# Sign words of the weight conversion formed on GpSimd beside VectorE's operations on h

## The chip, the cores and the metric

The kernel runs on one core of a Trainium2 chip. The metric is the device time of one execution in microseconds (us); the median of three runs is given. Engines are named as in the profile: PE is TensorE, PEld its weight load, DVE is VectorE, ACT is ScalarE, POOL is GpSimd, SP is SyncE, which here only issues DMAs.

## The reference

Linear attention over 8 batches and 8 heads, an RMS norm, and a feed-forward layer whose activation is a rational function:

```
kv = einsum('bhsd,bhse->bhde', k, v);  out = einsum('bhsd,bhde->bhse', q, kv)
x  = (out / sqrt(mean(out^2) + 1e-6) * g_norm)  -> 4608 x 512, float32
h  = x @ w_in                          # 512 -> 2048
P  = a0 + a1*h + a2*h^2 + a3*h^3
Q  = 1 + |b0|*|h| + |b1|*h^2
y  = (P / (Q + 1e-6)) @ w_out          # 2048 -> 512
```

The activations are float32, but `w_in` and `w_out` arrive as float64. They reach the chip as pairs of 32-bit words and are turned into float32 there.

## The kernel before

**Tiles and slots.** The 4608 tokens are cut into 9 tiles of 512 (`t`), the 2048 hidden columns into 16 chunks of 128 (`c`). One pair (t, c) is a slot, and the loop over `slots` (line 594) runs through all 144, tile by tile; slot i of tile 0 is chunk i. The order within each engine's queue is the order in which the code issues the instructions (`manual_schedule`). In a slot the first product of the next slot (`gemm1`, h), the second product of the slot two before (`gemm2`, into `acc`) and a piece of the next tile's attention (`att_kv`, `att_o`, ...) are issued for PE, and the rational function of the slot itself for ACT and DVE.

**The rational function.** For a slot, `ew_a` has ACT write d = h^2 (L427), q = |b0 h| (L428) and u (L430), and DVE form q (L429, the denominator) and u (L431, times h). `ew_b` has DVE go on with u and h (L437), while ACT takes d = exp(-ln q) (L438, L439). `ew_c` corrects the quotient on DVE: L443 (q and d), L445 (u and d), L451 (the result g). `ew_b` and `ew_c` take a `fill` function, by which other DVE work is placed between their operations: `fill(-1)` stands ahead of L437, `fill(0)` behind L443, `fill(2)` behind L451. The h that these read lies in PSUM, everything else in SBUF. In tile 0 the products are plain float32, so `ew_d` (the split of g into two parts, L461 and L462) does nothing there.

**The weight conversion.** The weights come in 16 units of two chunks each (`schedule`, line 125: the slot of the fetch, of `conv_a`, of `conv_b`, of the split). `conv_a` on ACT scales the high word, read as float32, by 2^-112, and the low word by 2^-29 (L183), both in place. `conv_b` on DVE makes the float32: `conv_b1` (L197) shifts the high word left by 3, `conv_b2` puts the sign bit of the high word back (L202) and adds the scaled low word as an integer (L203). Three units are converted ahead of the loop or in slot 0, in halves (`part`). The other 13 are converted whole, one in each of the slots 1 to 13: L197 stands at `fill(-1)`, between L431 and L437, and L202 and L203 at `fill(0)`, behind L443. The code of one slot of the loop around it:

```
        for u in at_slot(2, i):
            rest[-1].append(lambda u=u: conv_b1(u))
            rest[0].append(lambda u=u: conv_b2(u))
        ew_b(t, c, ph, lambda k: [f() for f in rest[k]])
```

**Names.** `raw_wi`, `raw_wo` are the fetched words, `wiw`, `wow` the float32 weights of tile 0 (`ups`), `parts`, `wil`, `wol` the two-part weights that the later tiles use (`split_w`, L224 and L231), `kvl` the small part of the kv matrix (L249), `op` the attention product (L327), `kvp` the kv product (L301).

Of the kernel before, what the change touches and what calls it, by code (L numbers as in the profile page):

```python
# [9 lines left out]
I32 = mybir.dt.int32  # L10
# [3 lines left out]
ALU = mybir.AluOpType  # L14
# [9 lines left out]
def linear_attention_then_rational_ffn(  # L24
# [13 lines left out]
    PE, ACT, DVE, POOL = nc.tensor, nc.scalar, nc.vector, nc.gpsimd  # L38
# [38 lines left out]
    b1abs = const.tile([P, 1], F32, name="b1abs")  # L77
# [41 lines left out]
    def f32(t):  # L119
        return t.bitcast(F32)  # L120
# [27 lines left out]
    def at_slot(step, k):  # L148
        return [u for u in units if schedule[u][step] == k]
# [7 lines left out]
    raws, ups, w32, whl, gparts = {}, {}, {}, {}, {}  # L157
# [15 lines left out]
    def words(u, part):  # L173
        w = raws[u].bitcast(I32).rearrange("p (f w) -> p f w", w=2)[:, part]
        return w[:, :, 0], w[:, :, 1]

    both, one, two = slice(0, 2 * DM), slice(0, DM), slice(DM, 2 * DM)
# [7 lines left out]
    def conv_a(u, part=both, engine="S"):  # L185
        low, high = words(u, part)
        scale(engine, f32(high), f32(high), 2.0**-112)
        scale(engine, low, low.bitcast(U32), 2.0**-29)

    def conv_b1(u, part=both):  # L190
        kind, c = u
        low, high = words(u, part)
        if u not in ups:
            ups[u] = wpool.tile([P, 2 * DM], F32, tag=f"f{units.index(u)}", name=f"{kind}w{c}")
            for j in range(2):
                w32[kind, c + j] = ups[u][:, j * DM:(j + 1) * DM]
        DVE.tensor_scalar(ups[u].bitcast(I32)[:, part], high, 3, None, ALU.logical_shift_left)  # L197

    def conv_b2(u, part=both):
        low, high = words(u, part)  # L200
        w = ups[u].bitcast(I32)[:, part]
        DVE.scalar_tensor_tensor(w, high, -(1 << 31), w, ALU.bitwise_and, ALU.bitwise_or)  # L202
        DVE.tensor_tensor(w, w, low, ALU.add)  # L203

    def conv_b(u, part=both):
        conv_b1(u, part)
        conv_b2(u, part)
# [6 lines left out]
    def split_w(u):  # L214
        kind, c = u
        i = units.index(u)
        w = ups.pop(u)
        if i == NU - 1:
            last = work.tile([P, 2 * DM], F32, tag="rb", name="w_last", bufs=2)
            DVE.tensor_copy(last, w)  # L220
            w = last
        fpart = lambda k, what: wpool.tile([P, 2 * DM], F32R, tag=f"f{k}", name=f"{kind}{what}{c}")
        wh = fpart(i - 1, "h") if i == NU - 1 else gpart((i + 1) // 2, (i + 1) % 2)
        ACT.copy(wh, w)  # L224

        def rest():
            wl = gpart(0, 0) if i == 0 else fpart(i if i == NU - 1 else i - 1, "l")
            for j in range(2):
                js = slice(j * DM, (j + 1) * DM)
                whl[kind, c + j] = wh[:, js], wl[:, js]  # L230
            DVE.tensor_tensor(wl, w, f32(wh), ALU.subtract)  # L231
        return rest
# [171 lines left out]
    def gemm1(t, c):  # L404
        ph = ps_h.tile([P, TW], F32, tag="h", name=f"h_{t}_{c}")
        gemm1_part(t, c, ph, slice(0, TW))
        return ph

    def gemm1_part(t, c, ph, cs):
        for kc in range(NPAIR):  # L410
            ks = slice(kc * P, (kc + 1) * P)
            if t == 0:
                PE.matmul(ph, w32["wi", c][:, ks], x0[:, kc, cs], start=(kc == 0), stop=(kc == NPAIR - 1))  # L413
                continue
            xh, xl = (f[:, cs] for f in x[t][kc])
            wh, wl = (f[:, ks] for f in whl["wi", c])
            PE.matmul(ph, wh, xl, start=(kc == 0), stop=False)  # L417
            PE.matmul(ph, wl, xh, start=False, stop=False)  # L418
            PE.matmul(ph, wh, xh, start=False, stop=(kc == NPAIR - 1))  # L419


    def ew_a(t, c, ph, w=TW):
        nm = f"{t}_{c}"
        d = work.tile([P, w], F32, tag="d", name=f"d_{nm}")
        q = work.tile([P, w], F32, tag="q", name=f"q_{nm}")
        u = work.tile([P, w], F32, tag="u", name=f"u_{nm}")
        ACT.activation(d, ph, AF.Square)  # L427
        ACT.activation(q, ph, AF.Abs, scale=b0)  # L428
        DVE.scalar_tensor_tensor(q, d, b1abs, q, ALU.mult, ALU.add)  # L429
        ACT.activation(u, ph, AF.Identity, bias=na[:, 2:3], scale=na[:, 3:4])  # L430
        DVE.tensor_tensor(u, u, ph, ALU.mult)  # L431
        pend[t, c] = (d, q, u)

    def ew_b(t, c, ph, fill=lambda k: None):
        d, q, u = pend[t, c]
        fill(-1)
        DVE.scalar_tensor_tensor(u, u, na[:, 1:2], ph, ALU.add, ALU.mult)  # L437
        ACT.activation(d, q, AF.Ln, bias=bias[:, 2:3], scale=QSC)  # L438
        ACT.activation(d, d, AF.Exp, bias=bias[:, 3:4], scale=-1.0)  # L439
# [14 lines left out]
    def ew_d(t, c, w=TW):  # L454
        u = pend.pop((t, c))[2]
        if (t, c) in gs:
            return
        nm = f"{t}_{c}"
        gh = work.tile([P, w], F32R, tag="gh", name=f"gh_{nm}")
        gl = work.tile([P, w], F32R, tag="gl", name=f"gl_{nm}")  # L460
        ACT.copy(gh, u)  # L461
        DVE.tensor_tensor(gl, u, f32(gh), ALU.subtract)  # L462
        gs[t, c] = (gh, gl)

    def gemm2(t, c, subs=range(NSUB)):
        g = gs.pop((t, c))
        c = int(c)
        if c == 0:
            acc[t] = [ps_acc.tile([P, DM], F32, tag="acc", name=f"acc_{t}_{s}") for s in range(NSUB)]
        for k, s in enumerate(subs):  # L470
            ss = slice(k * P, (k + 1) * P)
            o = acc[t][s]
            if unsplit(t, c):
                PE.matmul(o, g[:, ss], w32["wo", c], start=(c == 0), stop=(c == NF - 1))  # L474
                continue
            gh, gl = g
            wh, wl = whl["wo", c]
            PE.matmul(o, gl[:, ss], wh, start=(c == 0), stop=False)  # L478
            PE.matmul(o, gh[:, ss], wl, start=False, stop=False)  # L479
            PE.matmul(o, gh[:, ss], wh, start=False, stop=(c == NF - 1))  # L480

    def evacuate(t):
        for k in range(NSUB // 2):
            ob = work.tile([P, 2, DM], F32, tag="rb", name=f"ob_{t}_{k}", bufs=2)
            for s in range(2):
                ACT.copy(ob[:, s], acc[t][2 * k + s])
            r0 = t * TW + 2 * k * P
            nc.sync.dma_start(out[r0:r0 + 2 * P].rearrange("(s p) d -> p s d", s=2), ob)
# [101 lines left out]


    slots = [(t, c) for t in range(NTILE) for c in range(NF)]
    ph = gemm1(0, 0)
    for i, (t, c) in enumerate(slots[:-1]):
        ew_a(t, c, ph)
        if i:
            ew_d(*slots[i - 1])
        rest = {-1: [], 0: [], 1: [], 2: []}
        if i == 0:
            rest[0].append(lambda: conv_b(units[2], two))  # L600
        for u in at_slot(2, i):
            rest[-1].append(lambda u=u: conv_b1(u))
            rest[0].append(lambda u=u: conv_b2(u))
        ew_b(t, c, ph, lambda k: [f() for f in rest[k]])
        for u in at_slot(3, i):
            rest[2].append(split_w(u))
        for u in at_slot(1, i):
            conv_a(u)
        if i >= LAG:
            gemm2(*slots[i - LAG])  # L610
            if slots[i - LAG][1] == NF - 1:
                evacuate(slots[i - LAG][0])
        if i < 4:
            ph = gemm1(0, i + 1)
        if t + 1 < NTILE:
            for step, p in (attention0 if t == 0 else attention)[c]:
                todo_dve = step(t + 1, p)
                if todo_dve:
                    rest[2 if t == 0 else fillat[step]].append(todo_dve)
            for u in at_slot(0, i):  # L620
                fetch_w(u)
        if 4 <= i < len(slots) - 2:
            ph = gemm1(*slots[i + 1])
        if c == NF - 2 and t < NTILE - 1:
            xl = [split(t + 1, p) for p in range(NPAIR)]
            for k in range(2):
                rest[k].append(xl[k])
                rest[2].append(xl[2 + k])
        ew_c(t, c, lambda k: [f() for f in rest[k]])
# [43 lines left out]
```

## Time and profile before

| | |
|---|---|
| median of three runs | 917.49 us (917.32 to 918.82) |
| the profiled execution | 916.91 us, of it the span 915.1 us |
| PE busy | 900.0 us (98%) |
| DVE busy | 800.3 us (87%) |
| ACT busy | 685.6 us (75%) |
| POOL busy | 4.8 us (1%), all of it in the first 20 us |
| granted PE clock | 1.00 throughout |

Busy PE is not PE at its peak: a matmul's end is modelled, and instructions that follow each other overlap by some tenths of a microsecond. So the time from one instruction's start to the next one's is the better measure of a step, on DVE too. The chain of waits is followed back from the last instruction; where an engine stands in it, that engine set the pace.

### The profile page before, as it was taken

To read this page: it belongs to the slowest core of one execution; us is meant where nothing else is said; L and a number is where in the kernel's file an instruction comes from. 1 tells how busy PE (TensorE), PEld (TensorE's weight loads), DVE (VectorE), ACT (ScalarE), POOL (GpSimd) and SP (SyncE) were. 2 spreads that over 40 slices of the span, in tenths; PEclk is the share of its full clock that TensorE was granted. 3 is DMA by queue.
4 is the path that set the end of the run, shared out by engine and by line. 5 is a ranking of instruction groups with operands and counts; after the bars stand their busy time and mean duration, and the time that the engine had idled before them with its cause. 6 is when DMAs were issued, how large, how long until landed. Compare 5 with 4: busy or idle time off the path is not lost.

```text
span 915.1 us, 11641 instructions
## 1 busy us (share of the span) xinstructions
PE 900.0 (98%) x4292; PEld 680.5 (74%) x4292; DVE 800.3 (87%) x1251; ACT 685.6 (75%) x1163; POOL 4.8 (1%) x32
## 2 busy tenths in 40 slices
PE   7999999999999999999999999999999999999998
PEld 5444445777678788878887888788887888788886
DVE  3799999999988899889987997889878988898887
ACT  2687866988687778777877787678867787777665
POOL 2000000000000000000000000000000000000000
PEclk9999999999999999999999999999999999999999
DMA  8945101322032013212221213110311020101001
GB/s 321 368 178 218 35 24 41 96 72 48 1 127 71 20 39 103 65 41 47 87 81 41 48 41 124 44 48 29 98 52 48 0 69 13 48 1 46 1 1 46
DMA packets 24416, 65.89 MB, mean 72 GB/s; under 512 B 2792, under 2 KB 2792, under 8 KB 24360
## 3 DMA queue, kind: packets, MB, share of 16 engines
q1 hardware_dynamic: 23328, 64.10, 21.5%
q10 hardware_dynamic: 1032, 1.05, 0.3%
q8 instruction: 33, 0.54, 0.3%
q14 instruction: 23, 0.19, 0.1%
HBM read 55.58 MB, written 9.57 MB: 71 GB/s over the span
## 4 chain that ended last, share of the span: by engine, by line
PE 83%; DVE 11%; ACT 3%; issue 1%; DMA 1%; DVEq 0%; ACTq 0%
PE h L417 13%; PE h L419 12%; PE h L418 12%; PE acc L478 12%; PE acc L479 11%; PE acc L480 11%; PE acc L474 3%; PE h L413 2%; PE kvp L301 2%; DVE q L429 1%; DVE u L445 1%; DVE q L443 1%; PE idle L532 1%; DVE u L437 1%; PE ms L345 1%
## 5 line engine op out<-in xcount | busy, mean ns | idle before, releaser
L427 ACT ACTIVATE d<-h 128x512 f32<-128x512 f32 x143 | 85.8, 600 | 160.5 <-PE h L419 146.7
L417 PE MATMUL h<-x,parts 128*128 128x512 f32 (+1 forms) x516 | 205.7, 399 | 0.0
L419 PE MATMUL h<-x,parts 128*128 128x512 f32 (+1 forms) x516 | 200.5, 389 | 0.0
L479 PE MATMUL acc<-wol,gh 128*128 128x512 f32 x492 | 191.5, 389 | 0.7 <-DVE wol L231 0.7
L429 DVE SCALAR_TENSOR_TENSOR q<-d,b1abs,q 128x512 f32<-128x512 f32 x143 | 107.1, 749 | 81.3 <-ACT q L428 81.1
L418 PE MATMUL h<-x,wil 128*128 128x512 f32 (+1 forms) x452 | 175.5, 388 | 0.0
L478 PE MATMUL acc<-parts,gl 128*128 128x512 f32 x440 | 171.6, 390 | 0.2 <-DVE gl L462 0.2
L480 PE MATMUL acc<-parts,gh 128*128 128x512 f32 x440 | 171.2, 389 | 0.0
L438 ACT ACTIVATE d<-q,bias 128x512 f32<-128x512 f32 x143 | 105.2, 735 | 29.8 <-DVE q L429 28.8
L417 PEld LDWEIGHTS h<-x,parts 128*128 128x128 f32 x516 | 96.9, 188 | 26.3 <-DVE gl L462 5.0
L419 PEld LDWEIGHTS h<-x,parts 128*128 128x128 f32 x516 | 96.9, 188 | 20.6
L430 ACT ACTIVATE u<-h,na 128x512 f32<-128x512 f32 x143 | 112.2, 784 | 0.0
L479 PEld LDWEIGHTS acc<-wol,gh 128*128 128x128 f32 x492 | 92.3, 188 | 20.0 <-DVE wol L231 1.0
L439 ACT ACTIVATE d<-d,bias 128x512 f32<-128x512 f32 x143 | 103.5, 724 | 4.7
L445 DVE SCALAR_TENSOR_TENSOR u<-u,na,d 128x512 f32<-128x512 f32 x143 | 106.5, 745 | 0.0
L437 DVE SCALAR_TENSOR_TENSOR u<-u,na,h 128x512 f32<-128x512 f32 x143 | 106.0, 742 | 0.3
L443 DVE SCALAR_TENSOR_TENSOR q<-q,d 128x512 f32<-128x512 f32 x143 | 98.4, 688 | 1.3 <-ACT d L439 1.3
L431 DVE TENSOR_TENSOR u<-u,h 128x512 f32<-128x512 f32 x143 | 97.9, 684 | 0.9
L428 ACT ACTIVATE q<-h,ab 128x512 f32<-128x512 f32 x143 | 98.1, 686 | 0.0
L418 PEld LDWEIGHTS h<-x,wil 128*128 128x128 f32 x452 | 85.0, 188 | 16.2 <-issue 0.2
L478 PEld LDWEIGHTS acc<-parts,gl 128*128 128x128 f32 x440 | 82.6, 188 | 18.4 <-DVE gl L462 1.1
L480 PEld LDWEIGHTS acc<-parts,gh 128*128 128x128 f32 x440 | 82.6, 188 | 17.2
(136 smaller groups left out, 1089.8 us busy)
## 6 DMA issues: line engine op xcount, KB each, us to landing
kvm<-in_kv_dram SPq DMA_DIRECT2D x28, 640.0 KB
raw_wo<-in_w_out_dram SPq DMA_DIRECT2D x8, 1024.0 KB
qr<-in_qT_dram SPq DMA_DIRECT2D x32, 256.0 KB
out_dram<-ob SPq DMA_DIRECT2D x16, 512.0 KB
rb<-rd SPq DMA_DIRECT2D x28, 256.0 KB
raw_wi<-in_w_in_dram SPq DMA_DIRECT2D x6, 1024.0 KB
first<-in_first_dram SPq DMA_DIRECT2D x4, 640.0 KB
raw_wi<-in_w_in_dram SPq DMA_DIRECT2D x4, 512.0 KB
```

Source lines behind the costliest of these rows:

```text
L417: PE.matmul(ph, wh, xl, start=(kc == 0), stop=False)
L418: PE.matmul(ph, wl, xh, start=False, stop=False)
L419: PE.matmul(ph, wh, xh, start=False, stop=(kc == NPAIR - 1))
L429: DVE.scalar_tensor_tensor(q, d, b1abs, q, ALU.mult, ALU.add)
L430: ACT.activation(u, ph, AF.Identity, bias=na[:, 2:3], scale=na[:, 3:4])
L437: DVE.scalar_tensor_tensor(u, u, na[:, 1:2], ph, ALU.add, ALU.mult)
L438: ACT.activation(d, q, AF.Ln, bias=bias[:, 2:3], scale=QSC)
L443: DVE.scalar_tensor_tensor(q, q, QEPS, d, ALU.add, ALU.mult)
L445: DVE.scalar_tensor_tensor(u, u, na[:, 0:1], d, ALU.add, ALU.mult)
L478: PE.matmul(o, gl[:, ss], wh, start=(c == 0), stop=False)
L479: PE.matmul(o, gh[:, ss], wl, start=False, stop=False)
L480: PE.matmul(o, gh[:, ss], wh, start=False, stop=(c == NF - 1))
```

## The change

For the 13 units that are converted whole, the shift on DVE (L197) is gone. POOL multiplies the scaled high word, read as float32, by 0.0 (the product is a zero with the word's sign, that is, the sign bit alone) and writes it to the weight tile. DVE's L202 then shifts the high word by 3 and ors it with that in one operation (L209 of the changed kernel). A manual dependency makes the POOL operation wait until the slot's first DVE operation (L429, the denominator q; L436 in the changed kernel) is done. The units that are converted in halves stay as they were.

```diff
@@ conv_b1, conv_b2
-        DVE.tensor_scalar(ups[u].bitcast(I32)[:, part], high, 3, None, ALU.logical_shift_left)
+        if part != both:
+            DVE.tensor_scalar(ups[u].bitcast(I32)[:, part], high, 3, None, ALU.logical_shift_left)
+            return None
+
+        return POOL.tensor_scalar(ups[u], f32(high), 0.0, None, ALU.mult)
 
     def conv_b2(u, part=both):
         low, high = words(u, part)
         w = ups[u].bitcast(I32)[:, part]
-        DVE.scalar_tensor_tensor(w, high, -(1 << 31), w, ALU.bitwise_and, ALU.bitwise_or)
+        if part != both:
+            DVE.scalar_tensor_tensor(w, high, -(1 << 31), w, ALU.bitwise_and, ALU.bitwise_or)
+        else:
+            DVE.scalar_tensor_tensor(w, high, 3, w, ALU.logical_shift_left, ALU.bitwise_or)
         DVE.tensor_tensor(w, w, low, ALU.add)
@@ ew_a
-        DVE.scalar_tensor_tensor(q, d, b1abs, q, ALU.mult, ALU.add)
+        q_made = DVE.scalar_tensor_tensor(q, d, b1abs, q, ALU.mult, ALU.add)
         ...
+        return q_made
@@ the loop over slots
+    beside = mybir.DependencyInfo(mybir.DependencyClass.Sync, mybir.DependencyReason.DATA)
     ph = gemm1(0, 0)
     for i, (t, c) in enumerate(slots[:-1]):
-        ew_a(t, c, ph)
+        q_made = ew_a(t, c, ph)
+        for u in at_slot(2, i):
+
+            tc.add_manual_dep(conv_b1(u).ins, q_made.ins.name, beside, reason="signs beside h")
         ...
         for u in at_slot(2, i):
-            rest[-1].append(lambda u=u: conv_b1(u))
             rest[0].append(lambda u=u: conv_b2(u))
```

The order of instructions moves in two places. On DVE, slot 1 (the second chunk of tile 0, unit `wi` 4) stood so before, `wiw_372` being the weight tile and the names in `_1_` those of the slot:

```order
L429 SCALAR_TENSOR_TENSOR q_1_365<-d_1_364,b1abs,q_1_365 128x512
L431 TENSOR_TENSOR u_1_366<-u_1_366,h_1_348 128x512
L197 TENSOR_SCALAR wiw_372<-raw_wi_249 128x1024
L437 SCALAR_TENSOR_TENSOR u_1_366<-u_1_366,na,h_1_348 128x512
L443 SCALAR_TENSOR_TENSOR q_1_365<-q_1_365,d_1_364 128x512
L202 SCALAR_TENSOR_TENSOR wiw_372<-raw_wi_249,wiw_372 128x1024
L203 ISA wiw_372<-raw_wi_249,wiw_372 128x2048
L445 SCALAR_TENSOR_TENSOR u_1_366<-u_1_366,na,d_1_364 128x512
L451 SCALAR_TENSOR_TENSOR g_1_405<-q_1_365,u_1_366 128x512
```

One row leaves; nothing else on DVE changes its place, here and in the 12 other slots.

The same slot on DVE in the changed kernel, with the semaphores that each row waits for:

```order
L436 SCALAR_TENSOR_TENSOR q_1_365<-d_1_364,b1abs,q_1_365 128x512 [waits Activation_49]
L438 TENSOR_TENSOR u_1_366<-u_1_366,h_1_348 128x512 [waits Activation_49]
L445 SCALAR_TENSOR_TENSOR u_1_366<-u_1_366,na,h_1_348 128x512 [waits DVE_49]
L451 SCALAR_TENSOR_TENSOR q_1_365<-q_1_365,d_1_364 128x512 [waits Activation_49]
L209 SCALAR_TENSOR_TENSOR wiw_372<-raw_wi_249,wiw_372 128x1024 [waits DMAHW2_49,Pool_49]
L210 ISA wiw_372<-raw_wi_249,wiw_372 128x2048 [waits DVE_49]
L453 SCALAR_TENSOR_TENSOR u_1_366<-u_1_366,na,d_1_364 128x512
L459 SCALAR_TENSOR_TENSOR g_1_405<-q_1_365,u_1_366 128x512 [waits DVE_49]
```

The operation that shifts and ors now waits for POOL. On POOL, whose queue was empty behind `ghalf`, 13 operations stand now; the first five and the last of them:

```order
L566 TENSOR_SCALAR ghalf<-gcol 128x1 [waits DMAHW3_49,DMAHW1_49]
L201 TENSOR_SCALAR wiw_372<-raw_wi_249 128x1024 [waits DMAHW2_49,DVE_49]
L201 TENSOR_SCALAR wow_417<-raw_wo_255 128x1024 [waits DMAHW5_49,DVE_49]
L201 TENSOR_SCALAR wiw_464<-raw_wi_257 128x1024 [waits DMAHW6_49,DVE_49]
L201 TENSOR_SCALAR wow_513<-raw_wo_259 128x1024 [waits DMAHW7_49,DVE_49]
L201 TENSOR_SCALAR wiw_556<-raw_wi_353 128x1024 [waits DMAHW0_49,DVE_49]
L201 TENSOR_SCALAR wow_889<-raw_wo_674 128x1024 [waits DMAHW6_49,DVE_49,PE_49]
```

Each waits for DVE, and the last for PE too. The orders of PE, ACT and SP stay as they were; five fetches of later units on SP and five scalings on ACT also wait for POOL, since the raw words' buffers are read there now.

## Rows read from the trace of the kernel before

**Rows 1.** The page: busy time of each engine (share of the span, instructions), and the chain that ended last by engine.

```profile
PE 900.0 (98%) x4292; PEld 680.5 (74%) x4292; DVE 800.3 (87%) x1251; ACT 685.6 (75%) x1163; POOL 4.8 (1%) x32
...
PE 83%; DVE 11%; ACT 3%; issue 1%; DMA 1%; DVEq 0%; ACTq 0%
```

**Rows 2.** The chain that ended last in order of time, from 62 us to 198 us: start, duration (us), engine, tile and line.

```profile
62.12 0.69 DVE g L451
63.24 1.24 PE op L327 x4
...
95.75 3.45 PE h L413 x8
...
145.50 1.14 DVE parts L231
...
197.40 0.50 PE acc L478
```

**Rows 3.** The timeline of PE, the two places in tile 0's stretch where it sat idle on DVE: start, duration (us), line, operation, shapes, and in brackets the idle time before and what ended it.

```profile
63.24 1.24 PE L327 MATMUL op<-qr,kvf 128*128 128x64 f32 x4 [1.95 <-DVE kvl L249]
...
146.78 0.47 PE L418 MATMUL h<-x,parts 128*128 128x512 f32 x1 [1.53 <-DVE parts L231]
```

**Rows 4.** The timeline of DVE: slot 1 up to L202, then L429 and L443 of the slots 2 and 3.

```profile
41.40 0.75 DVE L429 SCALAR_TENSOR_TENSOR q<-d,b1abs,q 128x512 f32<-128x512 f32 x1
42.06 0.68 DVE L431 TENSOR_TENSOR u<-u,h 128x512 f32<-128x512 f32 x1
42.66 0.69 DVE L197 TENSOR_SCALAR wiw<-raw_wi 128x1024 int32<-128x1024 int32 x1
43.27 0.75 DVE L437 SCALAR_TENSOR_TENSOR u<-u,na,h 128x512 f32<-128x512 f32 x1
43.92 0.69 DVE L443 SCALAR_TENSOR_TENSOR q<-q,d 128x512 f32<-128x512 f32 x1
44.53 1.22 DVE L202 SCALAR_TENSOR_TENSOR wiw<-raw_wi,wiw 128x1024 int32<-128x1024 int32 x1
...
48.80 0.75 DVE L429 SCALAR_TENSOR_TENSOR q<-d,b1abs,q 128x512 f32<-128x512 f32 x1
...
51.44 0.68 DVE L443 SCALAR_TENSOR_TENSOR q<-q,d 128x512 f32<-128x512 f32 x1
...
55.83 0.75 DVE L429 SCALAR_TENSOR_TENSOR q<-d,b1abs,q 128x512 f32<-128x512 f32 x1
...
58.35 0.69 DVE L443 SCALAR_TENSOR_TENSOR q<-q,d 128x512 f32<-128x512 f32 x1
```

**Rows 5.** The timeline of DVE: L429 and L443 of slot 0 and of slot 14, which have no L197 between them.

```profile
35.32 0.75 DVE L429 SCALAR_TENSOR_TENSOR q<-d,b1abs,q 128x512 f32<-128x512 f32 x1 [1.13 <-ACT q L428]
...
37.62 0.69 DVE L443 SCALAR_TENSOR_TENSOR q<-q,d 128x512 f32<-128x512 f32 x1 [0.15 <-ACT d L439]
...
139.20 0.75 DVE L429 SCALAR_TENSOR_TENSOR q<-d,b1abs,q 128x512 f32<-128x512 f32 x1
...
141.49 0.69 DVE L443 SCALAR_TENSOR_TENSOR q<-q,d 128x512 f32<-128x512 f32 x1 [0.16 <-ACT d L439]
```

**Rows 6.** The timeline of ACT: the logarithm and the exponential of slot 1.

```profile
42.18 0.72 ACT L438 ACTIVATE d<-q,bias 128x512 f32<-128x512 f32 x1 [0.78 <-DVE q L429]
42.94 0.72 ACT L439 ACTIVATE d<-d,bias 128x512 f32<-128x512 f32 x1
```

**Rows 7.** Groups of POOL's instructions by line and shape: busy time (us), mean ns of one, idle before (us).

```profile
L117 POOL MEMSET kvl<- 128x128 f32 x6 | 1.3, 218 | 0.1
...
L85 POOL MEMSET kvf<- 128x1024 f32 x1 | 1.0, 952 | 0.0
...
L76 POOL TENSOR_SCALAR na<-ab 128x4 f32<-128x4 f32 x1 | 0.5, 483 | 6.1 <-DMA ab<-in_a_dram 6.1
L558 POOL TENSOR_SCALAR ghalf<-gcol 128x1 f32<-128x1 f32 x1 | 0.2, 227 | 2.2 <-DMA gcol<-in_g_dram 2.2
```

**Rows 8.** The timelines of DVE and ACT: L429 of the slots 8 to 13, L443 of the first and the last of the five slots 9 to 13, and ACT's L428 of the slots 10 to 12.

```profile
92.59 0.75 DVE L429 SCALAR_TENSOR_TENSOR q<-d,b1abs,q 128x512 f32<-128x512 f32 x1 [0.25 <-ACT q L428]
...
100.43 0.75 DVE L429 SCALAR_TENSOR_TENSOR q<-d,b1abs,q 128x512 f32<-128x512 f32 x1 [0.65 <-ACT q L428]
...
102.97 0.69 DVE L443 SCALAR_TENSOR_TENSOR q<-q,d 128x512 f32<-128x512 f32 x1
...
107.78 0.68 ACT L428 ACTIVATE q<-h,ab 128x512 f32<-128x512 f32 x1
...
108.76 0.74 DVE L429 SCALAR_TENSOR_TENSOR q<-d,b1abs,q 128x512 f32<-128x512 f32 x1
...
114.65 0.68 ACT L428 ACTIVATE q<-h,ab 128x512 f32<-128x512 f32 x1
...
115.67 0.75 DVE L429 SCALAR_TENSOR_TENSOR q<-d,b1abs,q 128x512 f32<-128x512 f32 x1
...
121.51 0.68 ACT L428 ACTIVATE q<-h,ab 128x512 f32<-128x512 f32 x1
...
122.58 0.74 DVE L429 SCALAR_TENSOR_TENSOR q<-d,b1abs,q 128x512 f32<-128x512 f32 x1
...
130.89 0.75 DVE L429 SCALAR_TENSOR_TENSOR q<-d,b1abs,q 128x512 f32<-128x512 f32 x1
...
133.41 0.69 DVE L443 SCALAR_TENSOR_TENSOR q<-q,d 128x512 f32<-128x512 f32 x1
```

## The prediction

> **What bounds the kernel now.** I read the page first: PE stands in 83% of the chain that ended last, DVE in 11%, and POOL is all but unused [rows 1]. The change touches only the slots 1 to 13 of tile 0, so the second view is the chain in order of time over tile 0. The reader is to see who paces which stretch [rows 2]: DVE up to 62 us, PE from 63.24 us to the h that is made at 95.75 us, DVE again until L231 at 145.50 us, then a mixture of DVE and ACT, and from 197.40 us PE. Third, PE's timeline shows where DVE's lateness reaches PE: it sat idle 1.95 us at 63.24 us behind L249, and 1.53 us at 146.78 us behind L231 [rows 3]. So time taken off DVE counts in the slots 1 to 3 (first stretch) and 9 to 13 (second stretch), and not in 4 to 8, where PE is the later one. What is won by 146.78 us shifts everything behind it: no instruction there changes.
>
> **What one slot loses and gains.** In slot 1, L429 starts at 41.40 us, L431 at 42.06, L197 at 42.66, L437 at 43.27 [rows 4]: L197 holds up DVE by 0.61 us. That isn't the gain. L443, two operations on, needs d from ACT, and ACT takes the logarithm and the exponential of q only once L429 is done: they run from 42.18 us to 42.94 + 0.72 = 43.66 us [rows 6], while L443 starts at 43.92. Without L197, L443 would still wait for that. The slots 0 and 14 have no L197 there and show it: L443 starts 2.30 us (37.62 - 35.32) and 2.29 us (141.49 - 139.20) after L429, behind an idle DVE that ACT's L439 releases [rows 5]. With L197 it is 2.52 us in the slots 1 and 3 (43.92 - 41.40, 58.35 - 55.83) and 2.64 us in slot 2 (51.44 - 48.80) [rows 4]. So a slot gains 0.22 us, in slot 2 0.34 us. The other 0.3 to 0.4 us become a wait of DVE for ACT.
>
> **What is added.** Thirteen POOL operations on 128 x 1024 float32. No such operation stands in the trace. From below: the memsets of 128 x 128 and 128 x 1024 take 218 and 952 ns, 0.82 ns an element; a one-element TENSOR_SCALAR takes 227 ns [rows 7]. That makes 0.227 + 1023 x 0.82 = 1.07 us. With the 483 ns of the four-element one as the fixed part it is 1.32 us. From above: a memset only writes, this one also reads, and every second word at that. If reading cost as much again, it would be 0.483 + 2 x 1020 x 0.82 = 2.15 us. I take 1.07 us, as these are streams of the same length on the same engine, and keep 2.15 us for the range. A price below 1.07 us changes nothing, since it is hidden already: POOL can start when ACT does, 0.78 us after L429's start (42.18 - 41.40) [rows 4, 6], and is then done 1.85 us after it. L443 comes at 2.29 us, and L202, which waits for POOL, at 2.29 + 0.61 (44.53 - 43.92) [rows 4] = 2.90 us. The work that hides POOL is L431 and L437. Neither sits behind POOL's semaphore.
>
> Here a rule speaks against the change. POOL is busy for 4.8 us in all [rows 1], at the start, so no row can tell whether one holds up the other. The Trainium skill, "SBUF — State Buffer", section "Who interferes with whom", says that a DVE instruction with two SBUF inputs contends with a GpSimd instruction that reads SBUF: the first has the shared ports for its whole length, and the other is blocked. By it L443 (q and d, both in SBUF) can't run until POOL is done, while L431 and L437 (u in SBUF, h in PSUM) can; without it only L202 would have to wait. At 1.07 us both give the same sum, and they part from 1.48 us on (2.29 - 0.78 - 0.03), which is the second rival.
>
> L202 keeps its form (two words in, one out, 1.22 us), with a shift in place of a mask: 0. The waits for POOL on SP's fetches and on ACT's scalings end before waits that were there already, since the same buffers are read by L202 and L203 afterwards: 0. The last POOL operation waits for PE to be done with a tile that was last read in slot 8, and it is issued in slot 13: 0.
>
> **The sum.** First stretch: 0.22 + 0.34 + 0.22 = 0.78 us earlier at L249, and PE was idle for 1.95 us there, so it follows. PE's stretch to 99 us: nothing more. Second stretch: DVE's L429 of slot 9 comes 0.78 us earlier with PE's h. Its L443 stood at 2.54 us (102.97 - 100.43), that of slot 13 at 2.52 (133.41 - 130.89), the five are alike [rows 8]: 0.25 us in slot 9, and 0.23 us in each of the others. But PE doesn't follow here, so the next L429 can't start before h and ACT's L428 allow. L428 ends at 108.46, 115.33 and 122.19 us, 0.30, 0.34 and 0.39 us ahead of the L429s at 108.76, 115.67 and 122.58 [rows 8]; I take 0.04 us of that for the way from engine to engine (from the end of L429 at 42.15 us to L438 at 42.18 it is 0.03 [rows 4, 6]). So at most 0.26, 0.30 and 0.35 us more can be had by the slots 10, 11 and 12. Slot 9 gives 0.25, slots 10 and 11 bring it to the 0.35 us that is to be had, slots 12 and 13 add 0.23 each, together 0.81 us. At 146.78 us PE was idle for 1.53 us on DVE [rows 3] and is itself 0.78 us earlier, so that it still waits for L231 and takes the whole: 0.78 + 0.81 = **1.6 us**. The profiled execution took 916.91 us, which makes 915.3; it lies 0.58 us under the median of 917.49, so I predict **915.9 us** for the median, 0.17% less. The smallest change that a measurement of this kernel can tell from none is about 0.2%, or 1.83 us (915.66 and 919.32 are the bounds).
>
> **The rivals.**
> - **POOL blocks L443.** If a POOL operation takes over 1.48 us, and L443 can't run beside it, L443 starts at 0.78 + p + 0.03 us instead of 2.29. The gain is gone at p = 1.71 us. With 2.15 us L443 comes at 2.96 us, 0.44 us later than with L197 (0.32 in the slots 2, 4, 6 and 8, which I take to be alike). First stretch 1.20 us; slots 4 to 8 1.84 us less the 0.90 us that DVE was idle ahead of L429 in the slots 8 and 9 [rows 8]; second stretch 5 x 0.43. Sum 4.3 us: 921.8 us, slower. For it: POOL's read of every second word has no row. Against it: POOL's own rows give 1.07 to 1.32 us. Chance 0.16. It is also what the page "GPSIMD Engine Reference", section "Elementwise — side-by-side cycle accounting" of the Trainium skill, would bring near: by its 2.6 cycles an element the operation is an estimated 2.2 us, though it states that for two inputs; no row here shows it.
> - **POOL is hidden only in part**: p between 1.5 and 1.9 us, as half way between the ends. With 1.6 us L443 starts at 2.41 us, and the eight slots that count gain 0.11 us each, 0.9 us at most; with 1.9 us they lose 0.19 us (0.07 in slot 2), some 1.4 us. Around 917.2 us, no change that can be told. Chance 0.19.
> - **The whole of L197 comes off**, because ACT's two operations don't hold L443. Three times 0.61 us is 1.8 us in the first stretch (PE's wait of 1.95 us allows it), and 0.35 + 0.61 + 0.61 in the second: 3.4 us, 914.1 us. Against it stand the waits of the slots 0 and 14 [rows 5]. Chance 0.07.
> - That the change doesn't do what it says would be a POOL operation that doesn't start behind L429. The order shows each of them waiting for DVE, so I give it nothing of its own.
>
> **How the numbers follow.** The forecast has 0.58. It lies 0.24 us inside the bound of 0.2%, and its terms (start times read to some hundredths, in eight slots, and what is lost or found between 147 and 197 us) carry some 0.7 us either way: 0.30 of it falls on faster, 0.28 on no change. Full gain 0.07 is faster. Hidden in part, 0.19, is no change. Blocked, 0.16, is slower. Faster 0.37, same 0.47, slower 0.16. The range runs from the full gain, 914.0, to 919.2 us, a POOL operation of 1.9 us with the spread of the runs; the blocked case is what is left out.
>
> **What would show it.** Right: POOL's operations of 1.0 to 1.4 us, each starting within 0.1 us of the end of L436 (the former L429); L451 (the former L443) 2.3 us behind L436 in the slots 1 to 13, ended by a wait for ACT's exponential; PE's wait for the former L249 down from 1.95 to about 1.2 us; L231 1.6 us earlier. Wrong: L451 starting where POOL ends; the shift-and-or taking longer than 1.22 us, or waiting for POOL; PE idle anywhere between 64 and 140 us.

## The result, and the profile after

The changed kernel takes 925.31 us (median of four runs, 924.77 to 926.10) against 917.67 us for the kernel before in the same comparison: a ratio of 1.0086, with a 95% interval from 1.0073 to 1.0098. It was forecast 0.17% faster, and it is 0.86% slower. The profiled execution took 926.10 us, of it a span of 924.3.

Lines have moved: L429 is now L436, L431 L438, L437 L445, L443 L451, L202 L209, L203 L210, L249 L256, L231 L238, and POOL's new operation is L201. The page after, to be set beside [rows 1]; busy time of each engine, then the chain that ended last:

```profile
PE 903.8 (98%) x4292; PEld 682.3 (74%) x4292; DVE 795.9 (86%) x1238; ACT 684.9 (74%) x1163; POOL 42.4 (5%) x45
...
PE 77%; DVE 4%; ACT 3%; issue 1%; POOLq 0%; DVEq 0%; ACTq 0%
```

DVE lost its 13 operations (1251 to 1238), as the diff says, and 4.4 us of busy time. POOL gained 13 and 37.6 us. The groups of POOL's instructions (busy us, mean ns of one, idle before):

```profile
L201 POOL TENSOR_SCALAR wow<-raw_wo 128x1024 f32<-128x1024 f32 x7 | 20.0, 2864 | 37.5 <-DVE q L436 31.4 <-issue 6.1
L201 POOL TENSOR_SCALAR wiw<-raw_wi 128x1024 f32<-128x1024 f32 x6 | 17.3, 2876 | 52.0 <-DVE q L436 47.3 <-DMA raw_wo<-in_w_out_dram 4.7
```

One takes 2.87 us. What that does to a slot is seen in the timeline of DVE in slot 1 (start, duration, line, operation, shapes, idle before), which answers to [rows 4]:

```profile
40.56 0.74 DVE L436 SCALAR_TENSOR_TENSOR q<-d,b1abs,q 128x512 f32<-128x512 f32 x1
41.22 0.68 DVE L438 TENSOR_TENSOR u<-u,h 128x512 f32<-128x512 f32 x1
41.94 0.75 DVE L445 SCALAR_TENSOR_TENSOR u<-u,na,h 128x512 f32<-128x512 f32 x1
42.85 0.69 DVE L451 SCALAR_TENSOR_TENSOR q<-q,d 128x512 f32<-128x512 f32 x1 [0.16 <-ACT d L447]
44.29 1.23 DVE L209 SCALAR_TENSOR_TENSOR wiw<-raw_wi,wiw 128x1024 int32<-128x1024 int32 x1 [0.75 <-POOL wiw L201]
```

and of POOL beside it:

```profile
41.38 2.87 POOL L201 TENSOR_SCALAR wiw<-raw_wi 128x1024 f32<-128x1024 f32 x1 [27.14 <-DVE q L436]
```

POOL starts 0.82 us behind the start of L436 and runs until 44.25. L451 comes 2.29 us behind L436, released by ACT's exponential, beside a POOL that is still running, and is not stretched (0.69 us). The operation that shifts and ors waits for POOL: it starts 3.73 us behind L436, where L202 started 3.13 us behind L429 (44.53 - 41.40) [rows 4]. That happens in all 13 slots, 9.8 us of waits in the stretch of tile 0 (waited for: sum, times, longest):

```profile
DVE wow L209 <- POOL wow L201: 5.3, 7, 0.8
DVE wiw L209 <- POOL wiw L201: 4.5, 6, 0.8
```

Over the slots 1 to 13, L209 stands 0.47 to 0.68 us later behind its slot's first operation than L202 did, 7.5 us in all. PE has to wait for that, and something more follows. PE's timeline, to be set beside [rows 3]:

```profile
64.13 2.29 PE L334 MATMUL op<-qr,kvf 128*128 128x64 f32 x4 [3.07 <-DVE kvl L256]
66.22 5.60 PE L420 MATMUL h<-x,wiw 128*128 128x512 f32 x8
...
150.80 0.50 PE L424 MATMUL h<-x,parts 128*128 128x512 f32 x1 [1.89 <-DVE x L279]
...
153.89 0.77 PE L425 MATMUL h<-x,parts 128*128 128x512 f32 x1 [2.59 <-DVE parts L238]
```

The idle time ahead of `op` has grown from 1.95 to 3.07 us, and the same four matmuls behind it take 2.29 us instead of 1.24 [rows 3]. The eight of h behind them take 5.60 us; in the kernel before they took 3.60 at the same place:

```profile
64.32 3.60 PE L413 MATMUL h<-x,wiw 128*128 128x512 f32 x8
```

The windows of the changed kernel show why (stretch, length, busy us of PE, PEld, DVE, ACT and POOL with counts, granted PE clock, DMA share, GB/s):

```profile
62.00:63.00 1.00, 0.00 (x0) 0.00 (x0) 0.98 (x2) 0.85 (x2) 0.00 (x0) 1.00 0.00 0
63.00:64.00 1.00, 0.00 (x0) 0.00 (x0) 0.97 (x3) 0.00 (x0) 0.00 (x0) 0.71 0.00 0
64.00:65.00 1.00, 0.87 (x3) 0.87 (x4) 0.94 (x3) 0.10 (x1) 0.06 (x1) 0.50 0.00 0
...
70.00:71.00 1.00, 1.00 (x3) 0.38 (x2) 0.98 (x2) 0.00 (x0) 0.00 (x0) 0.88 1.02 422
...
153.00:154.00 1.00, 0.11 (x1) 0.14 (x1) 1.00 (x2) 0.32 (x1) 0.00 (x0) 0.50 0.00 0
...
159.00:160.00 1.00, 1.00 (x3) 0.43 (x3) 0.24 (x1) 1.00 (x2) 0.00 (x0) 1.00 0.00 0
```

The granted clock falls from 1.00 to 0.50 (from 2.4 to 1.2 GHz) in the idle time and stays there until 70 us, and once more from 152 to 159 us. In the profiled execution of the kernel before it stood at 1.00 through both places; e_memset below shows that this is not so in every execution.

The starts of the slots' first operations, L429 or L436, give an account that leaves out what differs ahead of the loop. How much later than in the kernel before each place comes, counted from the first operation of slot 0 (us; all rows but the first are runs of the next section):

| | slot 4 | slot 5 | slot 9 | slot 14 | end of the span |
|---|---|---|---|---|---|
| after | 1.73 | 3.58 | 4.85 | 7.95 | 10.04 |
| e_warm2 (clock kept up) | 1.73 | 2.23 | 3.53 | 6.69 | 7.07 |
| e_nosign (no POOL operation) | -0.80 | -1.13 | -0.79 | -1.59 | -1.58 |
| e_behind (consumer moved back) | -0.80 | -1.13 | -0.79 | -1.59 | -1.06 |
| e_unread (before, with a POOL result nobody reads) | 1.76 | 2.29 | 3.69 | 7.01 | 7.82 |
| e_memset (before, with POOL memsets) | -0.02 | 0.53 | 1.69 | 1.68 | 1.67 |

### The profile page after: what moved, and what is told of

It is laid out like the page before. It is cut to its first block, busy times and chain, and to the rows that moved or that the text cites. A ratio compares the mean times of both kernels' runs of the same rounds, so it can differ in the third digit from the quotient of the medians.

```text
span 924.3 us, 11676 instructions
## 1 busy us (share of the span) xinstructions
PE 903.8 (98%) x4292; PEld 682.3 (74%) x4292; DVE 795.9 (86%) x1238; ACT 684.9 (74%) x1163; POOL 42.4 (5%) x45
## 4 chain that ended last, share of the span: by engine, by line
PE 77%; DVE 4%; ACT 3%; issue 1%; POOLq 0%; DVEq 0%; ACTq 0%
PE h L424 13%; PE h L425 12%; PE h L426 12%; PE acc L486 11%; PE acc L487 11%; PE acc L488 11%; PE acc L482 2%; PE kvp L308 2%; PE ms L352 1%; PE op L339 1%; PE op L340 1%; PE op L338 1%; ACT parts L231 1%; DVE q L436 0%; DVE u L453 0%
## 5 line engine op out<-in xcount | busy, mean ns | idle before, releaser
L436 DVE SCALAR_TENSOR_TENSOR q<-d,b1abs,q 128x512 f32<-128x512 f32 x143 | 107.1, 749 | 83.3 <-ACT q L435 83.0
L437 ACT ACTIVATE u<-h,na 128x512 f32<-128x512 f32 x143 | 112.0, 783 | 0.0
L445 DVE SCALAR_TENSOR_TENSOR u<-u,na,h 128x512 f32<-128x512 f32 x143 | 106.1, 742 | 0.7
L451 DVE SCALAR_TENSOR_TENSOR q<-q,d 128x512 f32<-128x512 f32 x143 | 98.4, 688 | 2.9 <-ACT d L447 2.8
L438 DVE TENSOR_TENSOR u<-u,h 128x512 f32<-128x512 f32 x143 | 97.8, 684 | 0.9
```

The lines of the kernel that those rows point to most:

```text
L436: q_made = DVE.scalar_tensor_tensor(q, d, b1abs, q, ALU.mult, ALU.add)
```

## The experiments

The theory after the result: POOL's operation is dear of itself, L209 is the one that waits, and the longer idle time of PE costs clock on top. The rivals: DVE's side was misread too; or POOL is slow only because it meets DVE; or POOL holds up DVE's operations, so that even an unread result would cost.

**POOL's own price: e_quiet.** Four such operations ahead of the loop. The first two read every second word (`pairs`), the others words in a row. DVE is idle during the first and the last of them; the two between met its operations.

```diff
...
+    POOL.memset(probe, 0.0)
+    pairs = probe.rearrange("p (f w) -> p f w", w=2)[:, :, 1]
+    POOL.tensor_scalar(probed[:, 0:512], pairs, 0.0, None, ALU.mult)
+    POOL.tensor_scalar(probed[:, 0:256], pairs[:, 0:256], 0.0, None, ALU.mult)
+    POOL.tensor_scalar(probed[:, 0:512], probe[:, 0:512], 0.0, None, ALU.mult)
+    POOL.tensor_scalar(probed, probe, 0.0, None, ALU.mult)
```

> The kernel before with four extra POOL operations of the change's kind at its start, where DVE is idle, on a zeroed scratch tile: 512 and 256 words with every second one read, then 512 and 1024 words side by side. In the change one of 1024 took 2.87 us beside DVE. If that is POOL's own price, 512 take about 1.4 to 1.5 us here and 256 half of that, and stride decides nothing or the contiguous ones are faster by their reads. If DVE held POOL up, 512 take about 0.65 us here (0.227 + 511 x 0.82 ns).

POOL's groups by shape (busy us, mean ns of one, idle before):

```profile
L129 POOL TENSOR_SCALAR probed<-probe 128x1024 f32<-128x1024 f32 x1 | 2.8, 2768 | 0.1
L126 POOL TENSOR_SCALAR probed<-probe 128x512 f32<-128x512 f32 x1 | 1.5, 1529 | 0.1
L128 POOL TENSOR_SCALAR probed<-probe 128x512 f32<-128x512 f32 x1 | 1.5, 1488 | 0.1
...
L127 POOL TENSOR_SCALAR probed<-probe 128x256 f32<-128x256 f32 x1 | 1.0, 1007 | 0.0
```

The operation costs 2.77 us by itself: (2768 - 1488) / 512 = 2.5 ns a word and about 0.2 us fixed. Every second word (L126) costs no more than words in a row (L128). So it is the price of the operation, neither DVE nor the stride. The 256 words took 1.01 us and not half of 1.5; this one started beside DVE's operations, so it tells no price. L128 met DVE too, and there it was DVE that paid. L212, the addition of the low word in this run (two inputs in SBUF), takes 1.11 us beside it; the unit before it, without POOL, had 0.69:

```profile
14.97 1.49 POOL L128 TENSOR_SCALAR probed<-probe 128x512 f32<-128x512 f32 x1
```

```profile
15.02 1.11 DVE L212 CUSTOM_DVE_ANT_0 wiw<-raw_wi,wiw 128x1024 uint16<-128x1024 uint16 x1
```

The time, 916.33 us in its one run, tells nothing at this size.

**DVE's side alone: e_nosign.** The POOL operation is left out and L209 takes the high word twice, so the sign handling of the 13 units is missing; DVE's order is that of the changed kernel.

```diff
-        return POOL.tensor_scalar(ups[u], f32(high), 0.0, None, ALU.mult)
+        return None
...
-            DVE.scalar_tensor_tensor(w, high, 3, w, ALU.logical_shift_left, ALU.bitwise_or)
+            DVE.scalar_tensor_tensor(w, high, 3, high, ALU.logical_shift_left, ALU.bitwise_or)
...
```

> The change with POOL's 13 operations left out: the sign words are not made, and L209 (same form, same length) takes the high word in their place, so the weights of the 13 units lose their sign handling. It measures DVE's side of the prediction by itself. Theory A (DVE's side was right, POOL's was not): L451 2.3 us after L436 in the slots 1 to 13, L209 right behind it, clock 1.00, 1.6 us less than before: 915.9 us (915.4 to 916.4). Rival: the gain per slot is not had even without POOL (PE or ACT takes it), 917.5 us.

915.06 us, a ratio of 0.9973 [0.9962, 0.9983]. L451 in slot 1 and PE at the first place:

```profile
43.77 0.69 DVE L451 SCALAR_TENSOR_TENSOR q<-q,d 128x512 f32<-128x512 f32 x1 [0.16 <-ACT d L447]
44.38 1.22 DVE L209 SCALAR_TENSOR_TENSOR wiw<-raw_wi 128x1024 int32<-128x1024 int32 x1
```

```profile
62.52 1.24 PE L334 MATMUL op<-qr,kvf 128*128 128x64 f32 x4 [1.23 <-DVE kvl L256]
```

L436 stood at 41.48, so L451 comes 2.29 us behind it; PE's wait is 1.23 us ("about 1.2" was predicted); the loop is 0.80 us earlier by slot 4 and 1.59 by slot 14, where the prediction had 0.78 and 1.6. DVE's side was not misread. By the medians the lead is larger, 2.9 us (917.99 - 915.06); e_memset has the likely rest.

**Half the words: e_half.** POOL on the first 512 columns only; L209 still waits for it but takes the high word twice, so the sign handling is missing here too.

```diff
+        return POOL.tensor_scalar(ups[u][:, one], f32(high)[:, one], 0.0, None, ALU.mult)
...
```

> The change with POOL's operation on the first half of the columns only (512, about 1.5 us), L209 in its old place and still waiting for it, but taking the high word instead of the sign words; the sign handling of the 13 units is left out. Only POOL's length changes. Theory A: POOL ends 2.3 us after L436's start, L209 wants it at 2.9 us and doesn't wait; 915 us, as e_nosign (914.5 to 916). Rival B: as the POOL operation itself costs, some half of the 7.8 us stays, 919 to 922 us.

915.38 us, 0.9977 [0.9967, 0.9987]. POOL and L209 in slot 1:

```profile
42.03 1.59 POOL L201 TENSOR_SCALAR wiw<-raw_wi 128x512 f32<-128x512 f32 x1 [27.74 <-DMA raw_wi<-in_w_in_dram]
```

```profile
44.10 1.22 DVE L209 SCALAR_TENSOR_TENSOR wiw<-raw_wi 128x1024 int32<-128x1024 int32 x1
```

POOL is done at 43.62 us, and L209 stands right behind L451 without a wait. The prediction's mechanism holds at a price that is hidden.

**Start POOL earlier: e_free.** The manual dependency goes, so that POOL runs as soon as ACT has scaled the word, a slot earlier.

```diff
-            tc.add_manual_dep(conv_b1(u).ins, q_made.ins.name, beside, reason="signs beside h")
+            conv_b1(u)
```

> The change without the manual dependency: POOL's operation starts as soon as ACT has scaled the unit's high word, one slot earlier. Theory A (the sign words come late: POOL takes 2.87 us instead of the 1.07 us of the prediction, DVE waits 0.75 us for them in each of 13 slots, and the longer idle of PE lets the clock fall to half twice): POOL is done before L209 wants its words, L209 waits for nothing, L451 comes 2.3 us after L436, the clock stays at 1.00, and the 1.6 us of the prediction are had: 915.3 to 916.3 us. Theory B (POOL and DVE block each other at the ports): POOL now runs beside operations with two SBUF inputs (L209, L210, L451, L453), so either these take or are held 0.5 us or more per slot, 920 us and up, or POOL's operation stretches to well over 3 us.

925.87 us, 1.0097 [1.0082, 1.0113]: nothing won, and the rival saw it. L209 waits no longer, but POOL now starts during it, and the next operation pays. DVE and POOL in slot 1:

```profile
44.87 1.22 DVE L209 SCALAR_TENSOR_TENSOR wiw<-raw_wi,wiw 128x1024 int32<-128x1024 int32 x1
46.12 2.02 DVE L210 CUSTOM_DVE_ANT_0 wiw<-raw_wi,wiw 128x2048 uint16<-128x2048 uint16 x1
```

```profile
45.36 3.43 POOL L201 TENSOR_SCALAR wow<-raw_wo 128x1024 f32<-128x1024 f32 x1 [3.52 <-ACT raw_wo L183]
```

L210 takes 2.02 us instead of 1.22. POOL's 13 operations now start in the slots 0 to 12, and in each of them L210 is stretched by 0.8 to 0.9 us, about as much as the wait that went.

**The same, with the consumers moved up: e_free_up.** L209 and L210 also move ahead of L445 (`rest[-1]`), into the time in which DVE waits for ACT.

```diff
-            rest[0].append(lambda u=u: conv_b2(u))
+            rest[-1].append(lambda u=u: conv_b2(u))
```

> As e_free, and the two operations L209 and L210 stand ahead of L445 instead of behind L451, so that DVE has work while ACT takes the logarithm and the exponential. If the part of L197's 0.61 us that the prediction gave up (0.3 to 0.4 us per slot) was lost to that wait alone, no DVE operation waits for ACT's exponential in the slots 1 to 13 and the whole 0.61 us comes off in the slots that count: about 914.1 us, 1.5 to 2 us less than e_free. If the wait is not what costs it (DVE's pace is set elsewhere), the time is that of e_free within 0.5 us.

916.20 us, 0.9986 [0.9977, 0.9995]: 9.7 us less than e_free, and 2.1 us more than the 914.1 that were expected. Slot 1:

```profile
45.09 1.22 DVE L210 CUSTOM_DVE_ANT_0 wiw<-raw_wi,wiw 128x2048 uint16<-128x2048 uint16 x1
46.23 0.74 DVE L445 SCALAR_TENSOR_TENSOR u<-u,na,h 128x512 f32<-128x512 f32 x1
46.89 0.93 DVE L451 SCALAR_TENSOR_TENSOR q<-q,d 128x512 f32<-128x512 f32 x1
```

```profile
45.98 3.03 POOL L201 TENSOR_SCALAR wow<-raw_wo 128x1024 f32<-128x1024 f32 x1 [3.52 <-ACT raw_wo L183]
```

Now L445, with one input in SBUF and one in PSUM, stands behind POOL's start and isn't stretched, and L451 loses only 0.24 us (0.24 to 0.31 in the slots 1 to 12). The two runs fit one account: POOL's operation waits until the DVE operation that ran before it is done (46.09 in e_free, 46.31 here; less that wait it takes 2.70 us in both), and then holds up a DVE operation with two inputs in SBUF until about 0.8 us behind that point. L210 of e_free ends 1.22 us behind 46.92, that is 46.09 + 0.83; L451 here ends 0.69 us behind 47.13, that is 46.31 + 0.82. The other 1.9 us of POOL's operation hold up nothing.

**A result nobody reads: e_unread.** The kernel before, and POOL's multiplication in two halves into a scratch tile, released by L429.

```diff
...
+                made = POOL.tensor_scalar(signs, f32(high)[:, half], 0.0, None, ALU.mult)
+                tc.add_manual_dep(made.ins, q_made.ins.name, beside, reason="signs beside h")
```

> The kernel before, with POOL's 13 operations added (as two halves of 512 columns each, released by L429 as in the change) that write to a scratch tile which nobody reads; DVE keeps L197 and L202. Theory A: POOL beside DVE costs nothing by itself, 917.5 us within 0.5, DVE's rows as before, L443 2.52 us after L429. Theory B: L443 (two SBUF inputs) starts only when a POOL operation ends, or POOL's running stretches DVE's operations: 0.4 us per slot or more, 920 us and up.

924.72 us, 1.0086 [1.0073, 1.0098]: a miss for the theory, as nothing waits for these operations. DVE and POOL in slot 1 (L438 and L444 are L437 and L443 of before here):

```profile
42.65 0.79 DVE L197 TENSOR_SCALAR wiw<-raw_wi 128x1024 int32<-128x1024 int32 x1
...
44.01 1.16 DVE L444 SCALAR_TENSOR_TENSOR q<-q,d 128x512 f32<-128x512 f32 x1
```

```profile
42.21 1.69 POOL L602 TENSOR_SCALAR signs<-raw_wi 128x512 f32<-128x512 f32 x1 [28.05 <-DVE q L429]
...
43.98 1.53 POOL L602 TENSOR_SCALAR signs<-raw_wi 128x512 f32<-128x512 f32 x1
```

The second half starts at 43.98, just ahead of L444, which takes 1.16 us instead of 0.69: 0.47 us for 512 words (0.42 in e_quiet), against 0.80 for 1024 in e_free. It is so in all 13 slots, only that in slot 5 it is L202 that is held. L197, with one input, in SBUF, is stretched too, by 0.02 to 0.20 us a slot, beside the first half. Here the third rival holds: by slot 14 the loop is 7.01 us late, so the placing of POOL's start costs as much as the wait does in the changed kernel (6.69 in e_warm2). The clock fell to 0.50 at the same two places here as well.

**Writes alone: e_memset.** The same with POOL's memsets.

```diff
-                made = POOL.tensor_scalar(signs, f32(high)[:, half], 0.0, None, ALU.mult)
+                made = POOL.memset(signs, 0.0)
```

> e_unread with POOL memsets (two of 512 columns per slot into the unread scratch, released by L429) in place of the multiplications: POOL writes, but reads nothing. Theory A (it is POOL's reads that hold up DVE's operations with two SBUF inputs): L443 and L202 have their lengths and starts of before, 917.5 us within 0.7. Rival: POOL's writes hold them up as well, L197 or L443 is stretched as in e_unread, 920 us and up.

918.25 us, 1.0005 [0.9996, 1.0014]. DVE in slot 1:

```profile
41.99 0.69 DVE L197 TENSOR_SCALAR wiw<-raw_wi 128x1024 int32<-128x1024 int32 x1
...
43.25 0.68 DVE L444 SCALAR_TENSOR_TENSOR q<-q,d 128x512 f32<-128x512 f32 x1
```

Nothing is stretched. It is POOL's reading that holds up DVE, which the memset rows of [rows 7] could not show.

This execution shows something else besides. PE waited for L249 as long as in the kernel before, 1.94 us, and here the clock fell to 0.50, from 63.6 to 67.0 us:

```profile
62.56 1.30 PE L327 MATMUL op<-qr,kvf 128*128 128x64 f32 x4 [1.94 <-DVE kvl L249]
```

```profile
66.00:67.00 1.00, 1.00 (x2) 0.34 (x1) 1.00 (x1) 1.00 (x2) 0.00 (x0) 0.50 0.99 373
```

The loop is level with the kernel before by slot 4 and 1.7 us late from slot 9 to the end, so this fall cost 1.7 us. The other executions of the kernel before fit that. Of the 27 in this comparison, 13 have a mean granted clock of 0.994 or 0.998 and a span of 916.0 to 916.9 us, 14 have 0.996 or 1.000 and a span of 914.3 to 915.4. (A fall in the first 15 us, which takes 0.004 off the mean in e_behind, would explain why the two groups interleave.) Where the clock fell in them is not recorded. All executions of e_nosign, whose PE waits 1.23 us there, stand at 0.996 or 1.000. So about half of the executions of the kernel before likely hold such a fall, and what e_nosign wins beyond its 1.59 us is likely that.

**The clock: e_warm and e_warm2.** The changed kernel with matmuls on zeros into an unused PSUM tile: 12 ahead of slot 4's `op`, 7 and 10 around the first matmul of tile 1's h. e_warm read the constant zero tile, e_warm2 a zero tile of its own.

```diff
...
+            if t == 1 and c == 0 and kc == 0:
+                warm(7, idle15, zero2)
             PE.matmul(ph, wh, xl, start=(kc == 0), stop=False)
+            if t == 1 and c == 0 and kc == 0:
+                warm(10, idle15, zero2)
...
+        if i == 4:
+            warm(12, ps_at.tile([P, TW], F32, tag="ms", name="idle4", bufs=1), zero2)
```

> The change as it is, and 29 unneeded 128 x 128 matmuls into a free PSUM bank in PE's two long waits (12 ahead of the attention product of slot 4, 7 and 10 around the first product of tile 1), some 2.8, 1.7 and 2.4 us of work. Theory A (part of the loss is the clock, which fell to 0.50 from 63.7 to 70 us and from 152.6 to 159 us): the clock stays at 1.00 after 30 us, 1.8 us come back at the first place and 2.4 us at the second, 925.3 less 4.2 makes 921 us (920.5 to 922). If the clock costs nothing, as DVE is late anyway, the time stays at 925 us.

e_warm took 927.27 us, 1.0108 [1.0095, 1.0122]. It tells of the clock only up to slot 8, where it was 1.3 us ahead of the changed kernel; then a wait of its own came. The matmuls share a buffer and a zero tile with the attention work, and ACT waited 4.78 us for PE:

```profile
104.71 0.60 ACT L343 ACTIVATE sq<-op 128x512 f32<-128x512 f32 x1 [4.78 <-PE ms L352]
```

> e_warm with a zero tile of its own for the dummy matmuls (in e_warm they read a buffer that the attention tiles rotate through, and ACT had to wait 4.8 us at slot 8 for them). Theory A: the clock stays at 1.00 in both places; at slot 5 this is worth 1.3 us, as in e_warm up to slot 8, and 2.4 us at the second place: 921.6 us (921 to 922.5). If the clock costs nothing: 925 us.

e_warm2 took 923.64 us, 1.0065 [1.0051, 1.0078]. The windows show the clock kept at 1.00 in both places, with PE busy 9.62 us of ten:

```profile
60.00:70.00 10.00, 9.62 (x43) 5.86 (x42) 8.69 (x12) 7.87 (x15) 3.14 (x2) 1.00 0.41 149
150.00:160.00 10.00, 9.62 (x61) 6.68 (x61) 9.73 (x15) 6.53 (x12) 0.00 (x0) 1.00 0.01 2
```

Between the medians that is 1.7 us (925.31 - 923.64), less than was expected (921 to 922.5 us); between the two profiled executions 3.0 us (10.04 - 7.07 in the table). So the clock is a real, smaller part, 1.7 to 3.0 us, and the other 6 to 7 us are DVE's waits: the 7.5 us of the 13 slots, less the 0.90 us that DVE was idle ahead of slots 8 and 9 [rows 8], is 6.6; e_warm2 shows 6.69 at slot 14.

**Give POOL its time: e_behind.** The change with one index different: L209 and L210 stand behind L459, the slot's result, instead of behind L451.

```diff
-            rest[0].append(lambda u=u: conv_b2(u))
+            rest[2].append(lambda u=u: conv_b2(u))
```

> The change with one thing moved: L209 and L210 stand behind L459 (fill(2)) instead of behind L451, so that POOL's 2.87 us are over before L209 wants its words, while POOL's start stays beside L438 and L445, which have one input in SBUF. Theory A (the change lost because POOL takes 2.87 us and its words are wanted 2.1 us after its start, and because POOL's reads, in their first 0.83 us only, hold up a DVE operation with two SBUF inputs): no DVE operation waits for POOL or is stretched, clock 1.00, and the time is that of e_nosign, 915 us (914.5 to 916.5). Rival B (POOL beside DVE costs something of its own wherever it stands, by ports or power): 918 us and up.

915.65 us, 0.9983 [0.9975, 0.9992]: faster than the kernel before and than the changed one, with all of the computation in it. DVE and POOL in slot 1:

```profile
43.25 0.69 DVE L451 SCALAR_TENSOR_TENSOR q<-q,d 128x512 f32<-128x512 f32 x1 [0.17 <-ACT d L447]
43.86 0.74 DVE L453 SCALAR_TENSOR_TENSOR u<-u,na,d 128x512 f32<-128x512 f32 x1
44.64 0.69 DVE L459 SCALAR_TENSOR_TENSOR g<-q,u 128x512 f32<-128x512 f32 x1
45.25 1.22 DVE L209 SCALAR_TENSOR_TENSOR wiw<-raw_wi,wiw 128x1024 int32<-128x1024 int32 x1
```

```profile
41.79 2.92 POOL L201 TENSOR_SCALAR wiw<-raw_wi 128x1024 f32<-128x1024 f32 x1 [27.02 <-DVE q L436]
```

POOL still takes 2.9 us, ends at 44.71, and L209 comes at 45.25 without waiting. By slots 4, 9 and 14 the loop is as far ahead as without any POOL operation. The wait for POOL, and the clock that it cost, were the whole loss.

**ACT instead of POOL: e_act_up and e_act_uf.** ACT writes the sign words, and L209 and L210 stand ahead of L445 as in e_free_up. The results are wrong, with a scale of 0.0 and with 2^-100 (e_act_uf); that ACT's copy drops the sign of a zero product would explain it, but no row shows the words.

```diff
...
-        return POOL.tensor_scalar(ups[u], f32(high), 0.0, None, ALU.mult)
+        return ACT.activation(ups[u], f32(high), AF.Copy, scale=0.0)
...
```

> The sign words from ACT instead of POOL (a copy with scale 0.0 behind the two scalings of the unit, one slot earlier, about 1.1 us), and L209 and L210 ahead of L445 as in e_free_up. No POOL operation is left to hold up DVE's operations with two SBUF inputs. Theory A (e_free_up still lost 0.25 to 0.33 us per slot at L451 to POOL's reads): 914.1 us, if ACT's 1.4 us of waiting per slot ahead of the logarithm cover the added 1.1 us. Rival: ACT is then the late one in the slots 1 to 8, its L435 holds L436 back, and the time is 916 us or more.

> e_act_up with a scale of 2^-100 instead of 0.0, so that the scaled high word underflows to a zero that may keep its sign (with 0.0 ACT's copy loses it). Nothing else changes: 915.5 us, as e_act_up (914.8 to 916.3), and a second version that beats the kernel before, if the sign is kept.

915.51 us, 0.9975 [0.9965, 0.9985], and 914.59 us, 0.9968 [0.9958, 0.9979]. An operation takes about 1.15 us on ACT, and in the slots 1 to 5 DVE then waits for ACT's q, up to 0.94 us (L438 is L429 of before here):

```profile
55.75 0.75 DVE L438 SCALAR_TENSOR_TENSOR q<-d,b1abs,q 128x512 f32<-128x512 f32 x1 [0.94 <-ACT q L437]
```

So the move frees DVE and loads ACT, which is next to set the pace. As the results are wrong, these times are bounds and no version to use.

## Why the prediction was wrong

**The step that failed is the price of POOL's operation.** "I take 1.07 us, as these are streams of the same length on the same engine" built it from memsets [rows 7]. It measured 2.87 us in the kernel and 2.77 us on its own (e_quiet). The upper bound of 2.15 us, reading at the memset's pace on top of writing, was too low as well: a multiplied word costs 2.5 ns, three times a written one (0.82 ns). The chances and the range stood on that bound. By the prediction's own figures POOL had until 2.90 us behind L436; starting at 0.78 + 0.03 it could take 2.09 us unnoticed. 2.87 - 2.09 = 0.78 us too much is, within some hundredths, the 0.75 us wait of L209.

**The page that was cited was nearer than the rows.** The Trainium skill, "GPSIMD Engine Reference", section "Elementwise — side-by-side cycle accounting", gave an estimated 2.2 us by its two-input figure of 2.6 cycles an element; the trace shows 2.87 us for one input. That figure too lies under the measurement.

**Who waits.** The rival with the right sign, "POOL blocks L443", had L451 held until POOL ends. It wasn't: it came 2.29 us behind L436, released by ACT, 1.47 us into POOL's operation. The waiter is the consumer, L209. The prediction listed "waiting for POOL" among what would show it wrong, but gave it no price. The rule behind that rival, the Trainium skill, "SBUF — State Buffer", section "Who interferes with whom", is half borne out. Two-input operations are held by a POOL that reads (L210 in e_free, L444 in e_unread), not by one that only writes (e_memset), and those with one input in SBUF and one in PSUM go free (L445). But POOL holds DVE for 0.8 us of its 2.9, not for its whole length. The measurement decides: by the whole length L210 of e_free would have ended near 50.0 (46.09 + 2.70 + 1.22), and it ended at 48.14.

**The omitted term.** The sum let a longer wait of PE cost only itself. It went from 1.95 to 3.07 us, and the clock fell to 0.50: 1.7 us by the medians of e_warm2. The same holds the other way round: at 1.94 us the clock can fall already (e_memset, 1.7 us), so that a shorter wait is likely worth more than the 1.6 us of the sum.

**What was right.** POOL's start (0.08 us behind the end of L436), the 0.22 us of a slot, ACT as what holds L451, and the sums of 0.78 and 1.6 us, which e_nosign gave as 0.80 and 1.59 and e_behind as 0.80 and 1.59 by the end of tile 0. That the whole of L197 could come off only if ACT's two operations didn't hold L451 was right for this order; e_free_up, which puts L209 and L210 into that wait, takes the wait away, and then pays for POOL's start in L451.

**Open.** The size of the clock's part (1.7 us by medians, 3.0 by two profiled executions), and why the clock fell behind 1.94 us in e_memset and not behind 1.95 us in the kernel before. That POOL reads its words in the first 0.8 us and computes afterwards is an inference from where DVE was held; no row shows the reads. Of POOL's operations only this multiplication and the memset were tried, and the stretch of L197 in e_unread was not followed up.

## What to carry to other kernels

Price an operation by a row of the same kind; a memset is no measure of one that also reads and computes, and if there is no such row the upper bound belongs far above the forecast, and the forecast on what happens there. When work goes to another engine, work out by when its consumer wants the result and place the consumer behind that time: here moving two operations behind the next two turned 0.86% lost into 0.17% won. Where an engine's start falls counts as much as its length: ahead of operations with one input in SBUF and one in PSUM POOL's was free, ahead of those with two in SBUF it cost as much as the wait.

## What the runs showed of the hardware that was not expected

- POOL's multiplication by a constant, float32, 128 partitions: 2.77 us for 1024 words, 1.49 for 512, 1.53 for 512 at a stride of two words (e_quiet).
- Beside it a DVE operation with two inputs in SBUF was held for about 0.8 us per 1024 words (e_free 0.80, e_free_up up to 0.82 behind POOL's start) and 0.42 to 0.47 for 512 (e_quiet, e_unread), at its start only; the other way round, POOL waited for the whole rest of a DVE operation that ran (0.73 us in e_free).
- After PE's idle 3.07 us the granted clock stood at 0.50 (1.2 GHz) for some 6 us, and again after 1.89 and 2.59 us close together. A wait of the same length went both ways: behind 1.95 us it stayed at 1.00 in the profiled execution of the kernel before [rows 3], behind 1.94 us it fell in e_memset, and the loop was 1.7 us later for it.
